# A fused attention and ELU kernel: relu from PSUM on VectorE, batch 2's exp tiles summed ahead of the row sums, and another order of the steps

## The chip, the cores and the metric

One NeuronCore of a Trainium2 chip runs the kernel. The metric is the device time of one execution in microseconds (us), smaller is better. The kernel before was run three times: 334.13, 334.70 and 338.02 us, median 334.7 us.

The core has these engines: TensorE (PE in the profile; its weight loads are PEld), VectorE (DVE), ScalarE (ACT), GpSimd (POOL) and SyncE (SP). PE multiplies from SBUF into PSUM. The others work on tiles of 128 partitions. POOL and SP issue the DMA transfers here. Each engine takes its instructions in the order in which they were issued to it.

## What is computed

Attention with 16 extra key and value rows per batch (the beacon), then a two-layer network with ELU over the result. Cut to what matters:

```python
# B, H, S, Nb, D = 8, 8, 576, 16, 64
k_all = np.concatenate([beacon_k, k], axis=2)
v_all = np.concatenate([beacon_v, v], axis=2)
scores = scale * np.matmul(q, k_all.transpose(0, 1, 3, 2))      # causal mask on the last S columns
a = np.exp(scores - scores.max(-1, keepdims=True))
a /= a.sum(-1, keepdims=True) + 1e-09
x = np.matmul(a, v_all).transpose(0, 2, 1, 3).reshape(B * S, H * D)   # 4608 x 512
h = x @ w_in                                                          # 4608 x 2048
g = np.where(h > 0.0, h, np.exp(np.minimum(h, 0.0)) - 1.0)            # ELU
out = g @ w_out                                                       # 4608 x 512
```

## The kernel before, in words

The kernel is a set of small functions, the steps, each marked `@step`, and one long string of step names that `run` (line 784) goes through from left to right. `F.2.11` calls `F(2, 11)`. A step only issues instructions. No scheduler moves them afterwards: the string is the order of every engine's queue, DMA queues included. Waits between engines follow from the data, from buffers that are used again, and from PSUM banks that two engines read.

**Attention**, per batch b (0 to 7) and pair p of heads (0 to 3). `lq` (line 247) loads q and k of batches 0 to 2 with POOL DMAs into the staging tiles `qst` and `kst`, of which there are two of each, taken in turn by even and odd batches. `T` transposes them on PE; `cq` and `ck` copy the result to SBUF on VectorE or ScalarE; `cb` puts the beacon's keys in front. From batch 3 on, `lk` (line 758) writes q and k in bf16 to a DRAM scratch, `lt` (line 763) brings them back transposed with SP DMAs, and `lp` (line 773) lets POOL write the beacon's keys into the same staging tile; `lp` therefore waits for the last reader of the batch that was in the tile before, and the POOL DMAs queued behind it wait with it. `lv` loads v, `wi` and `wo` load the two weights, all through POOL.

`S` computes transposed scores into PSUM, 512 columns a group; `x` (line 330) takes their exponential on ScalarE into the fp16 tile `et`; `m` multiplies masked blocks on VectorE. `L` (line 402) forms the row sums by multiplying `et` with a tile of ones: 20 matmuls of up to 464 columns over the five key blocks for the queries from 112 on, and 12 small ones for the first 112 queries and for half of their output. For batches 3 to 7 the step `D` (line 387) first adds the five key blocks of a pair of heads on VectorE, with four additions that shrink from 928 to 160 columns, into the `qk` tiles that `T` used before, and then `L` needs 4 matmuls in place of the 20. `n` turns the row sums into reciprocals on ScalarE (Ln, then Exp with scale -1), `W` multiplies with v, and `M` scales on VectorE into `xT`.

**Network.** Tokens are cut into tiles t: two of 256 tokens and eight of 512. `F` (line 503) multiplies `xT` with w_in into one PSUM bank `hps`, of which there are two in turn. The ELU of such a bank is done in one of two ways:

- `e`, `u`, `k`: ScalarE takes Exp of the bank (line 522) and Relu of the bank (line 527); VectorE forms min(exp - 1, relu) (line 537). This is ELU, as exp(h) - 1 is at least h.
- `e`, `r`, `g`: ScalarE takes Exp alone; VectorE forms min(exp, 1) - 1 in SBUF (`r`: line 545 for tiles 0 to 5, with a broadcast tile of ones, line 549 for tiles 6 and 7) and then the maximum with the bank in PSUM (`g`, line 554). This spares ScalarE the Relu.

`G` (tiles 0 and 1) and `Q` (tiles 2 to 9) multiply with w_out; `Q` uses Strassen's scheme, whose sums of weights and activations are `wt`, `H`, `Z` and, for the first product of tiles 8 and 9, `X`, `P`, `K`, `E`, `U` and `V`. `J` drains the sums from PSUM on either engine and writes the output through SP. `warm` and `wm` are matmuls on zeros, placed where PE has nothing to do yet.

Of the kernel before, what the change touches and what calls it, by code (L numbers as in the profile page):

```python
# [17 lines left out]
def kernel(  # L18
# [383 lines left out]
    def L(b, g):  # L402
# [12 lines left out]
        else:  # L415
            t = hd[b, g] = psum.tile([P, 1024], FP32, tag="S", name="lt")
            r_ = lt[b, g] = t[:, 512 - QA:512 - QA + S]
            if b >= BD:
                for i in range(4):
                    nc.tensor.matmul(  # L420
                        out=r_[32 * i:32 * (i + 1), QA:S], lhsT=ones,
                        rhs=presum[b, 2 * g + i // 2][:, i % 2, QA:S], start=True, stop=True, skip_group_check=True)
# [101 lines left out]
    @step  # L524
    def u(t, i):
        rb[t, i] = melt.tile([P, 512], FP16, tag="r", name="r")
        nc.scalar.activation(out=rb[t, i], in_=flat(hp[t, i]), func=AFT.Relu, bias=0.0, scale=1.0)  # L527
# [13 lines left out]
    @step  # L541
    def r(t, i):
        rb[t, i] = melt.tile([P, 512], FP16, tag="r", name="r")
        if t < 6:
            nc.vector.scalar_tensor_tensor(
                out=rb[t, i], in0=eb[t, i], scalar=1.0, in1=one32.to_broadcast([P, 512]),
                op0=ALU.min, op1=ALU.subtract)
# [393 lines left out]
```

## Time and profile before

| | us |
|---|---|
| median of three runs | 334.7 |
| profiled execution | 336.74 |
| its span, first to last instruction | 335.0 |
| DVE busy in it | 284.7 |
| ACT busy in it | 278.1 |
| POOL busy in it | 90.9 |

The profile is of one execution. Busy time is the time in which an engine worked on instructions; the end of a matmul in it is modelled. The page cuts the span in 40 slices of 8.4 us and shows the busy share in tenths. The chain of waits starts from the last instruction and follows back, at each step, to what released it. Groups collect instructions of one line with their mean duration; consecutive instructions of an engine overlap a little, so that a group's mean is slightly more than the step from one to the next. Of ELU steps, the kernel before has 120 `e`, of which 100 go on with `u` and `k` and 20 with `r` and `g`.

### The profile page before, as it was taken

The page shows a single profiled execution, that of the slowest core. Times are in us where ns is not written, and L with a number is a line of the kernel's source. Part 1 is how long each engine was busy: PE and PEld are TensorE (multiplying, and loading weights), DVE is VectorE, ACT ScalarE, POOL GpSimd, SP SyncE. Part 2 cuts the span into 40 slices and gives each one's busy share as a digit, 9 for nine tenths or more (in the row PEclk, how much of TensorE's full clock was granted, in tenths as well). Part 3 has the DMA queues.
Part 4 walks back from the last instruction along what each step waited for, and adds up shares of the span by engine and source line. Part 5 has one row for each costly group of instructions (what it writes and reads, how often), then busy time and mean ns, then how long its engine had stood idle before and what let it go on. Part 6 is the DMA issues. An engine that isn't in the chain of part 4 may idle for free.

```text
span 335.0 us, 8848 instructions
## 1 busy us (share of the span) xinstructions
PE 325.6 (97%) x3616; PEld 210.7 (63%) x3616; DVE 284.7 (85%) x601; ACT 278.1 (83%) x452; POOL 90.9 (27%) x117
## 2 busy tenths in 40 slices
...
GB/s 115 157 179 175 205 189 163 158 154 162 163 3 102 172 140 173 166 178 118 53 136 151 5 68 102 71 35 31 38 61 31 45 54 31 48 47 33 64 65 95
DMA packets 129113, 34.66 MB, mean 103 GB/s; under 512 B 112944, under 2 KB 127536, under 8 KB 129072
## 3 DMA queue, kind: packets, MB, share of 16 engines
...
## 4 chain that ended last, share of the span: by engine, by line
PE 87%; DVE 3%; ACT 3%; POOL 2%; DMA 2%; issue 1%; ACTq 0%; DVEq 0%; POOLq 0%
PE hps L512 30%; PE ops L627 29%; PE sc L321 8%; PE ut L378 6%; PE hps L697 5%; PE ops L563 4%; PE lt L378 2%; DMA kst<-in_k_dram 2%; ACT et L336 2%; POOL qst L136 1%; PE lt L420 1%; PE w L214 1%; PE tp L267 1%; PE ub L378 1%; DVE gt L554 1%
## 5 line engine op out<-in xcount | busy, mean ns | idle before, releaser
L512 PE MATMUL hps<-xT,w_in 128*128 128x512 f16 (+1 forms) x544 | 118.5, 354 | 0.3
L336 ACT ACTIVATE et<-sc 128x1024 f16<-128x1024 f32 (+2 forms) x114 | 105.7, 978 | 10.1 <-PE sc L321 9.5
L627 PEld LDWEIGHTS <-gt 128*128 128x128 f16 x768 | 73.3, 98 | 20.2 <-issue 3.7
L522 ACT ACTIVATE e<-hps 128x512 f32<-128x512 f32 x120 | 73.5, 620 | 13.8 <-PE hps L512 11.2
L512 PEld LDWEIGHTS <-w_in 128*128 128x128 f16 x544 | 50.6, 98 | 41.4 <-issue 4.4
L537 DVE SCALAR_TENSOR_TENSOR gt<-e,r 128x512 f16<-128x512 f32 x100 | 67.0, 684 | 8.0 <-ACT r L527 7.9
L527 ACT ACTIVATE r<-hps 128x512 f16<-128x512 f32 x100 | 61.9, 626 | 0.0
L627 PE MATMUL ops<-w_out,gt 128*128 128x256 f16 x384 | 50.7, 273 | 0.4 <-DVE gt L537 0.4
L627 PE MATMUL ops<-wt,gt 128*128 128x256 f16 x384 | 50.7, 273 | 0.0
L149 POOL DMA_DIRECT2D v<-in_v_dram x40 | 34.7, 919 | 5.0 <-DMA w_out<-in_moe_w_out_dram 2.7
L341 DVE TENSOR_TENSOR et<-et,triu 128x512 f16<-128x512 f16 (+4 forms) x108 | 31.2, 332 | 2.6 <-ACT et L336 2.4
L584 DVE TENSOR_TENSOR gt<-gt 128x1024 f16<-128x1024 f16 x48 | 32.4, 685 | 0.5
L378 PEld LDWEIGHTS <-v 128*32 128x32 f16 (+1 forms) x800 | 17.1, 96 | 10.6 <-issue 3.1
L394 DVE TENSOR_TENSOR qk<-qk,et 128x672 f16<-128x672 f16 (+2 forms) x60 | 21.2, 368 | 0.4
L378 PE MATMUL ut<-et,v 128*32 128x464 f16 (+3 forms) x560 | 20.9, 296 | 0.0
L472 DVE TENSOR_TENSOR xT<-ut,rl 128x672 f16<-128x672 f32 (+12 forms) x26 | 16.4, 670 | 3.1 <-PE ut L378 2.1
L643 DVE TENSOR_TENSOR osb<-ops,sm 128x512 f32<-128x512 f32 x24 | 16.4, 683 | 2.0 <-PE ops L627 1.9
L627 PE MATMUL ops<-w_out,s 128*128 128x256 f16 x128 | 17.1, 273 | 0.0
L563 PE MATMUL ops<-w_out,gt 128*128 128x512 f16 x64 | 16.0, 380 | 0.0
L736 DVE SCALAR_TENSOR_TENSOR gt<-e,r 128x512 f16<-128x512 f32 x24 | 15.9, 684 | 0.1
L627 PEld LDWEIGHTS <-s 128*128 128x128 f16 x128 | 12.3, 98 | 3.1 <-issue 0.3
L554 DVE TENSOR_TENSOR gt<-hps,r 128x512 f16<-128x512 f32 x20 | 13.7, 687 | 0.7
...
## 6 DMA issues: line engine op xcount, KB each, us to landing
...
```

The source lines that it names most:

```text
L149: nc.gpsimd.dma_start(out=vt[b][r0:r0 + n, j, :, :], in_=v[b, :, ilo[j]:ilo[j] + n, :].rearrange("h s d -> s h d"),)
L321: nc.tensor.matmul(out=s[:, h, a - c0:e - c0], lhsT=t[D * h:D * (h + 1), 1, P * j:P * (j + 1)], rhs=t[D * h:D * (h + 1), 0, NB + qa + a - ...
L336: nc.scalar.activation(out=ets[b, d][:, :, a - EC2 * d:e - EC2 * d], in_=sc[b, g][:, :, a - c0:e - c0], func=AFT.Exp, bias=0.0, scale=SCALE)
L341: nc.vector.tensor_tensor(out=o, in0=o, in1=i, op=ALU.mult)
L378: nc.tensor.matmul(out=t[32 * i:32 * (i + 1), a - qa:e - qa], lhsT=ones[0:kc[j], :] if half is None else v16[0:kc[j], j, h, 32 * half:32 * ...
L512: nc.tensor.matmul(out=h[:, n_, :], lhsT=w_in16[:, cc, P * fc:P * (fc + 1)], rhs=xt[k][:, cc, a - TT * k:e - TT * k], start=(cc == 0), sto ...
L522: nc.scalar.activation(out=eb[t, i], in_=flat(hp[t, i]), func=AFT.Exp, bias=0.0, scale=1.0)
L527: nc.scalar.activation(out=rb[t, i], in_=flat(hp[t, i]), func=AFT.Relu, bias=0.0, scale=1.0)
L537: nc.vector.scalar_tensor_tensor(out=half(t, i), in0=eb[t, i], scalar=1.0, in1=rb[t, i], op0=ALU.subtract, op1=ALU.min)
L563: nc.tensor.matmul(out=ob[t, tb_], lhsT=gt[:, fc, P * tb_:P * (tb_ + 1)], rhs=w_out16[:, fc, :], start=(fc == 0), stop=(fc == NFC - 1))
L584: (nc.vector if eng == "v" else nc.gpsimd).tensor_tensor(out=o_, in0=a_, in1=b_, op=op_)
L627: nc.tensor.matmul(out=xy[t, n_][:, qd, :], lhsT=lw[:, P * qd:P * (qd + 1)], rhs=wt_[:, c, :], start=(first and qd == 0 and c == 0), stop= ...
```

## The change

**The second way of ELU.** `u` gets an argument for its engine. With `.v`, VectorE takes the relu of the bank in PSUM, and `k` goes on as before. In the new order 31 of the 118 `u` carry `.v`; two `r` and `g` are left, on tile 6, where there were 20. The special form of `r` for tiles 0 to 5 goes, and its tile of ones with it.

**Batch 2's sums.** `L` takes the short form wherever `D` has been called for the pair. The order calls `D` for pairs 0 and 1 of batch 2, so that one of batch 2's two `L` has the short form.

**The order** is another one throughout. What the prediction speaks of: at the start POOL issues `ident` and all four `lq.0` before `lv.0.2`, where `lv.0.2` and `ident` stood between the first two and the last two; there are 14 `wm.4` in place of 18; `lq.2` stands behind `lv.1.2.3.4` and `lp.3.0`, where it stood right behind `wo.0`; of the `J` that copy or drain for Strassen's sums 6 are on VectorE in place of 11; one of batch 2's copies after the transposes moves from VectorE to ScalarE.

```diff
-    one32 = konst.tile([P, 1], FP32)
-    nc.vector.memset(one32, 1.0)
...
-            if b >= BD:
+            if (b, 2 * g) in presum:
...
     @step
-    def u(t, i):
+    def u(t, i, eng="s"):
         rb[t, i] = melt.tile([P, 512], FP16, tag="r", name="r")
-        nc.scalar.activation(out=rb[t, i], in_=flat(hp[t, i]), func=AFT.Relu, bias=0.0, scale=1.0)
+        if eng == "s":
+            nc.scalar.activation(out=rb[t, i], in_=flat(hp[t, i]), func=AFT.Relu, bias=0.0, scale=1.0)
+        else:
+            nc.vector.tensor_scalar(out=rb[t, i], in0=flat(hp[t, i]), scalar1=0.0, scalar2=None, op0=ALU.max)
...
     def r(t, i):
         rb[t, i] = melt.tile([P, 512], FP16, tag="r", name="r")
-        if t < 6:
-            nc.vector.scalar_tensor_tensor(
-                out=rb[t, i], in0=eb[t, i], scalar=1.0, in1=one32.to_broadcast([P, 512]),
-                op0=ALU.min, op1=ALU.subtract)
-        else:
-            nc.vector.tensor_scalar(
-                out=rb[t, i], in0=eb[t, i], scalar1=1.0, scalar2=1.0, op0=ALU.min, op1=ALU.subtract)
+        nc.vector.tensor_scalar(
+            out=rb[t, i], in0=eb[t, i], scalar1=1.0, scalar2=1.0, op0=ALU.min, op1=ALU.subtract)
...
     run("""
-    warm.4 warm.4 lq.0.0.0.4 lq.0.1.0.4 lv.0.2 warm.4 wm.4 ident T.0.0.0 bt ck.0.0.0 wm.4
-    T.0.1.0 bk cb.0.2 cb.0.0 wm.4 lq.0.0.4.8 S.0.0.0 x.0.0.0 lq.0.1.4.8 T.0.0.1 lq.1.0.0.4 tri
...
-    wm.4 x.0.1.1 T.0.2.1 S.0.3.0 wm.4 wm.4 x.0.3.0 T.0.3.1 cq.0.2.1 cq.0.3.1 S.0.2.0 wi.0
-    S.0.2.3 x.0.2.0 wm.4 wm.4 x.0.2.3 wm.4 wm.4 m.0.0.0 m.0.2.0 m.0.1.0 S.0.3.1 x.0.3.1 wm.4
...
-    x.0.2.2 M.0.A.0 M.0.A.1 F.0.2 e.0.2 u.0.2 k.0.2 lv.0.3.4 S.1.5 x.1.5 m.0.2.2 S.1.0 F.0.1
...
-    S.1.8 F.1.5 k.0.4 H.1.0 e.0.6 r.0.6 x.1.8 wo.0 lq.2.0.4.8 g.0.6 G.0.1.0 e.1.5 r.1.5 g.1.5
-    S.1.12 x.1.12 lq.2.0.0.4 wo.1 S.1.9 x.1.9 F.1.2 lv.1.0.1 S.1.10 x.1.10 F.1.3 m.1.2.1 cb.2.1
-    wo.2 e.1.3 T.2.2.0 u.1.3 cq.2.2.0 T.2.1.0 ck.2.1.0 G.0.0.0 e.1.2 u.1.2 T.2.0.0 lv.1.2.3.4
...
+    warm.4 lq.0.0.0.4 lq.0.1.0.4 warm.4 ident warm.4 wm.4 lq.0.0.4.8 wm.4 wm.4 bt bk lq.0.1.4.8
+    T.0.0.0 T.0.1.0 ck.0.1.0 cb.0.2 lv.0.2 lq.1.0.0.4 wm.4 cb.0.0 cb.0.1 lv.0.0.1 cb.0.3
...
+    tri cq.0.2.0 T.0.2.1 cq.0.2.1 S.0.3.0 x.0.3.0 T.0.3.1 cq.0.3.1 S.0.2.0 x.0.2.0 wm.4 S.0.2.3
+    wm.4 wm.4 m.0.0.0 m.0.2.0 x.0.2.3 S.0.2.1 x.0.2.1 S.0.3.1 x.0.3.1 m.0.1.0 wm.4 S.0.3.2
...
+    M.0.A.0 S.0.2.2 wi.0 M.0.A.1 F.0.2 m.0.0.2 u.0.2.v x.0.3.3 x.0.2.2 e.0.2 m.0.2.3 S.1.0 x.1.0
...
+    lv.1.2.3.4 u.1.5.v S.1.9 x.1.9 k.1.5 lp.3.0 cb.2.1 lq.2.0.0.4 F.1.2 S.1.10 x.1.10 u.1.2.v
+    cb.2.3 e.1.2 F.1.3 lq.2.0.4.8 T.2.2.0 m.1.2.0 T.2.1.0 G.0.0.0 e.1.3 ck.2.1.0 cq.2.2.0 H.1.2
...
+    e.2.14 S.2.8 F.2.0 wt.4.0 D.2.0.0 x.2.8 F.2.9 u.2.0 e.2.0 k.2.0 u.2.9 e.2.9 G.0.0.3 lp.3.1
...
     """)
```

More of the change, by code (lines that the diff above doesn't have):

```diff
@@ new lines @@
+    T.2.0.0 T.2.3.0 wo.1 u.1.3 F.0.7 m.1.2.1 ck.2.0.0 k.1.3 ck.2.3.0 u.0.7.v G.0.0.1 S.2.0 S.2.1
+    m.1.3.0 x.2.0 x.2.1 m.1.0.1 k.1.2 m.1.1.0 m.1.3.1 G.0.1.1 m.1.0.0 F.1.0 wo.3 u.1.0.v S.2.3
+    e.0.7 lv.1.0.1 L.1.0 e.1.0 x.2.3 F.1.6 k.0.7 H.1.0 L.1.1 n.1.0 M.1.0.0 e.1.6 m.2.0.0 n.1.1
+    k.1.0 M.1.1.0 wo.2 G.0.1.2 cb.2.2 u.1.6 W.1.1 M.1.1.1 W.1.0 S.2.2 x.2.2 G.0.0.2 M.1.0.1
+    F.2.11 e.2.11 H.2.2 u.2.11.v k.1.6 F.2.6 e.2.6 lv.2.0.1 S.2.4 x.2.4 u.2.6.v S.2.5 k.2.11
+    x.2.5 F.2.8 e.2.8 lk.3.0 u.2.8.v wt.1.0 lk.3.1 k.2.6 F.2.14 u.2.14 wt.2.0 k.2.8 G.0.1.3
@@ new lines @@
+    G.1.0.1 F.2.3 S.3.1 e.2.3 W.2.0 x.3.1 S.3.4 wt.2.1 m.2.3.1 k.2.4 u.2.3 x.3.4 M.2.0.1 k.2.3
+    F.2.10 F.2.12 e.2.10 e.2.12 L.2.1 lv.3.0.1 u.2.10.v u.2.12 o.0.1 k.2.10 S.3.8 n.2.1 x.3.8
+    F.2.7 k.2.12 F.2.5 M.2.1.0 W.2.1 u.2.7.v S.3.2 u.2.5 e.2.5 Z.2.3.0 M.2.1.1 e.2.7 Q.2.0.7
+    x.3.2 F.3.5 lk.4.0 k.2.7 e.3.5 s.0.1 k.2.5 m.3.1.0 u.3.5.v Z.2.1.0 k.3.5 S.3.6 S.3.9 F.3.2
+    lk.4.1 F.3.8 x.3.6 e.3.2 m.3.0.1 x.3.9 u.3.2.v G.1.0.2 lp.4.0 S.3.5 x.3.5 Z.2.3.1 lt.4.0
+    lt.4.1 e.3.8 S.3.10 x.3.10 k.3.2 Q.2.7.14 Z.2.1.1 lv.3.2.3.4 G.1.0.3 u.3.8 S.3.0 F.3.1 o.1.0
@@ new lines @@
+    lk.5.0 x.3.0 e.3.1 F.3.0 D.3.1.0 S.3.12 x.3.12 S.3.11 u.3.1 x.3.11 s.0.0 m.3.0.0 Q.2.14.21
+    Q.2.21.28 J.2.0 lk.6.1 wt.3.1 u.3.0 k.3.8 F.3.14 Z.2.2.0 S.4.1 u.3.14 Z.2.2.1 Z.2.4.0 e.3.0
+    S.4.0 D.3.0.0 e.3.14 D.3.0.1 H.1.1 Q.2.28.35 Q.2.35.42 J.2.1 k.3.0 Z.2.4.1 Q.2.42.49 k.3.1
+    D.3.0.2 F.3.6 D.3.0.3 x.4.1 x.4.0 u.3.6 m.3.1.1 D.3.1.1 e.3.6 F.3.4 k.3.6 J.2.2.v Q.2.49.56
+    S.3.7 lp.4.1 e.3.4 D.3.1.2 u.3.4 k.3.4 m.3.3.0 x.3.7 m.3.3.1 m.3.2.0 S.4.3 F.3.9 e.3.9
+    k.3.14 u.3.9 wt.4.1 D.3.1.3 wt.3.0 x.4.3 Q.2.56.63 F.3.15 e.3.15 u.3.15 k.3.15 F.3.3 S.4.4
@@ new lines @@
+    x.4.4 e.3.3 W.3.0 L.3.0 u.3.3 n.3.0 D.3.3.0 D.3.3.1 Q.2.63.70 J.2.3 m.3.2.1 F.3.7 e.3.7
+    k.3.3 u.3.7 Q.2.70.77 Q.2.77.84 D.3.3.2 F.3.11 e.3.11 F.3.12 M.3.0.1 D.3.3.3 Q.2.84.91 k.3.9
+    J.2.4 u.3.11 S.4.12 u.3.12 M.3.0.0 e.3.12 x.4.12 D.3.2.0 Z.3.3.0 D.3.2.1 k.3.12 D.3.2.2
+    D.3.2.3 S.4.11 x.4.11 F.3.13 e.3.13 k.3.7 Q.2.91.98 F.3.10 L.3.1 J.2.5 u.3.13 k.3.13 n.3.1
+    k.3.11 M.3.1.0 W.3.1 M.3.1.1 m.4.3.1 Q.2.98.105 lk.5.1 F.4.3 e.3.10 m.4.1.0 S.4.2 lt.5.0
+    u.3.10 e.4.3 k.3.10 u.4.3.v Z.3.3.1 S.4.10 Q.2.105.112 J.2.6.v F.4.8 x.4.10 Z.3.1.1 x.4.2
@@ new lines @@
+    e.4.8 u.4.8.v F.4.6 e.4.6 k.4.3 S.4.6 Z.3.1.0 x.4.6 k.4.8 S.4.5 x.4.5 Q.3.0.7 u.4.6 lp.5.0
+    Q.3.7.14 Q.3.14.21 S.4.7 S.5.4 Z.3.2.1 Z.3.2.0 x.5.4 m.4.0.0 x.4.7 F.4.7 F.4.9 k.4.6 J.3.0
+    Q.3.21.28 u.4.9.v e.4.7 u.4.7.v m.4.0.1 e.4.9 k.4.7 Q.3.28.35 S.5.2 m.4.1.1 J.3.1 H.2.1
+    S.4.9 x.5.2 F.4.1 D.4.0.0 Z.3.4.0 x.4.9 F.4.2 u.4.1 e.4.1 u.4.2 e.4.2 D.4.0.1 Q.3.35.42
+    k.4.9 S.5.0 lk.6.0 S.5.3 m.4.3.0 Q.3.42.49 x.5.0 lt.6.0 F.4.4 x.5.3 Q.3.49.56 e.4.4 lt.5.1
+    k.4.1 F.4.5 k.4.2 J.3.2 S.4.8 lv.4 u.4.4.v S.5.1 lp.7.0 e.4.5 k.4.4 x.4.8 D.4.1.0 D.4.1.1
@@ new lines @@
+    D.4.0.2 D.4.1.2 Z.3.4.1 D.4.0.3 m.4.2.1 D.4.1.3 lp.5.1 u.4.5 k.4.5 x.5.1 m.5.0.0 F.4.10
+    m.4.2.0 u.4.10 Q.3.56.63 Q.3.63.70 F.4.12 u.4.12 L.4.0 S.5.5 D.4.3.0 Q.3.70.77 e.4.12 x.5.5
+    n.4.0 F.4.14 D.4.2.0 e.4.14 m.5.0.1 J.3.3 D.4.2.1 M.4.0.0 u.4.14 D.4.2.2 W.4.0 M.4.0.1 S.5.6
+    x.5.6 Q.3.77.84 F.4.15 e.4.10 S.5.10 k.4.12 x.5.10 D.4.3.1 u.4.15 D.4.2.3 W.4.1 D.4.3.2
+    m.5.1.1 D.4.3.3 k.4.10 e.4.15 L.4.1 n.4.1 D.5.0.0 J.3.4 D.5.0.1 m.5.1.0 F.4.0 e.4.0 M.4.1.1
+    M.4.1.0 Q.3.84.91 Q.3.91.98 D.5.0.2 D.5.1.0 J.3.5 F.4.13 u.4.0 S.5.12 x.5.12 k.4.0 S.5.7
@@ new lines @@
+    lp.6.0 x.5.7 e.4.13 Q.3.98.105 F.5.6 S.6.1 D.5.1.1 S.6.4 u.5.6 Q.3.105.112 k.4.14 k.4.15
+    lp.6.1 D.5.1.2 x.6.1 Q.4.0.7 lt.6.1 H.4.1 u.4.13.v J.3.6.v k.4.13 S.5.9 Q.4.7.14 D.5.0.3
+    F.4.11 m.5.2.0 e.5.6 Z.4.3.0 x.5.9 x.6.4 e.4.11 u.4.11.v F.5.11 k.4.11 D.5.1.3 S.5.8 Z.4.3.1
+    S.5.11 Q.4.14.21 x.5.8 Z.4.1.0 J.4.0 F.5.7 Z.4.1.1 lv.5 W.5.0 e.5.11 x.5.11 u.5.11 k.5.6
+    Z.4.2.1 lk.7.1 u.5.7 k.5.11 e.5.7 Z.4.2.0 m.5.3.0 H.2.0 k.5.7 lv.6 L.5.0 n.5.0 M.5.0.1 F.5.1
+    u.5.1 e.5.1 F.5.14 Q.4.21.28 k.5.1 e.5.14 Q.4.28.35 M.5.0.0 J.4.1 u.5.14 F.5.15 e.5.15
@@ new lines @@
+    S.6.0 Z.5.3.1 e.5.3 x.6.0 S.6.10 F.5.9 u.5.9.v x.6.10 D.6.1.0 Q.4.98.105 e.5.9 m.6.0.0
+    D.6.0.0 F.5.0 S.6.8 u.5.0 e.5.0 x.6.8 S.6.6 m.6.0.1 D.6.0.1 k.5.0 k.5.3 k.5.9 Q.4.105.112
+    x.6.6 m.6.1.1 F.6.6 F.6.11 e.6.11 u.6.11 e.6.6 u.6.6 Z.5.1.1 J.4.6 Q.5.0.7 Q.5.7.14 S.6.11
+    x.6.11 F.6.4 Z.5.3.0 k.6.11 D.6.1.1 k.6.6 e.6.4 u.6.4 Q.5.14.21 S.7.2 Z.5.1.0 k.6.4 x.7.2
+    S.6.12 F.6.5 e.6.5 u.6.5 D.6.1.2 x.6.12 m.6.3.0 F.6.15 e.6.15 J.5.0.v Q.5.21.28 Z.5.2.0
+    u.6.15 Q.5.28.35 S.7.4 x.7.4 S.6.7 x.6.7 F.6.7 J.5.1 e.6.7 u.6.7 m.6.3.1 F.6.14 k.6.15
@@ new lines @@
+    m.6.2.1 D.6.0.2 D.6.0.3 W.6.0 D.6.1.3 L.6.0 H.4.0 e.6.14 u.6.14 Z.5.2.1 Q.5.35.42 m.6.2.0
+    Z.5.4.0 k.6.14 k.6.5 n.6.0 M.6.0.0 M.6.0.1 k.6.7 F.6.9 e.6.9 u.6.9 F.6.10 e.6.10 Q.5.42.49
+    k.6.9 J.5.2.v Q.5.49.56 S.7.1 u.6.10 x.7.1 D.6.3.0 S.7.3 x.7.3 Z.5.4.1 F.6.3 e.6.3 F.6.0
+    e.6.0 u.6.0 Q.5.56.63 r.6.3 g.6.3 m.7.1.0 m.7.0.1 S.7.6 x.7.6 S.7.5 Q.5.63.70 F.6.8 D.6.2.0
+    x.7.5 k.6.0 e.6.8 u.6.8 F.6.1 e.6.1 u.6.1 k.6.8 J.5.3 S.7.0 x.7.0 k.6.1 S.7.9 D.6.2.1
+    D.6.3.1 D.6.3.2 D.6.2.2 F.6.13 e.6.13 u.6.13 Q.5.70.77 F.6.12 k.6.13 D.6.2.3 Q.5.77.84 F.6.2
@@ new lines @@
+    e.6.12 D.6.3.3 r.6.12 J.5.4 L.6.1 x.7.9 k.6.10 n.6.1 e.6.2 M.6.1.0 u.6.2 W.6.1 Q.5.84.91
+    Q.5.91.98 Q.5.98.105 g.6.12 Z.6.3.1 M.6.1.1 F.7.15 F.7.0 Q.5.105.112 e.7.15 J.5.5 m.7.0.0
+    lv.7 u.7.15 S.7.7 D.7.1.0 e.7.0 S.7.12 F.7.3 m.7.1.1 k.6.2 x.7.7 Q.6.0.7 D.7.0.0 u.7.0
+    Z.6.3.0 J.5.6 D.7.1.1 Z.6.1.0 x.7.12 Q.6.7.14 D.7.0.1 F.7.12 k.7.0 Q.6.14.21 e.7.3 u.7.3
+    D.7.1.2 J.6.0 e.7.12 S.7.11 u.7.12 S.7.10 x.7.10 k.7.3 F.7.10 F.7.2 Z.6.1.1 k.7.12 Q.6.21.28
+    e.7.10 u.7.10 k.7.15 Z.6.2.0 D.7.0.2 D.7.0.3 e.7.2 u.7.2 Z.6.2.1 s.1.0 k.7.2 Q.6.28.35
@@ new lines @@
+    D.7.1.3 x.7.11 F.7.7 Z.6.4.1 F.7.13 e.7.7 u.7.7 m.7.3.0 L.7.0 k.7.7 e.7.13 u.7.13 k.7.13
+    S.7.8 F.7.8 F.7.1 x.7.8 e.7.1 m.7.3.1 D.7.3.0 Q.6.35.42 J.6.1 Q.6.42.49 m.7.2.0 D.7.2.0
+    u.7.1 k.7.1 m.7.2.1 Q.6.49.56 Q.6.56.63 e.7.8 F.7.6 u.7.8 k.7.8 n.7.0 J.6.2 e.7.6 Q.6.63.70
+    Z.6.4.0 F.7.4 k.7.10 u.7.6 D.7.3.1 D.7.3.2 k.7.6 M.7.0.0 e.7.4 F.7.14 u.7.4 D.7.3.3
+    Q.6.70.77 F.7.5 J.6.3.v Q.6.77.84 k.7.4 e.7.14 D.7.2.1 u.7.14 e.7.5 u.7.5 Z.7.3.0 F.7.9
+    D.7.2.2 e.7.9 D.7.2.3 k.7.14 F.7.11 L.7.1 u.7.9 n.7.1 e.7.11 J.6.4 Z.7.3.1 u.7.11 W.7.0
@@ new lines @@
+    H.3.1 P.8.0.0 K.8.0.0 H.3.0 Q.6.84.91 Q.6.91.98 k.7.9 X.8.1 Q.6.98.105 k.7.5 P.8.0.1 M.7.1.0
+    X.8.2 k.7.11 X.8.4 P.8.0.2 Q.6.105.112 K.8.0.2 J.6.6 K.8.0.1 P.8.0.3 X.8.3 P.8.0.4 M.7.0.1
+    Q.7.0.7 K.8.0.3 K.8.0.4 J.6.5 U.8.0.1 E.8.0.1 U.8.0.4 P.8.0.5 P.8.0.6 E.8.0.6 Z.7.1.0
+    K.8.0.5 Q.7.7.14 E.8.0.4 U.8.0.6 Z.7.2.0 Q.7.14.21 J.7.0 P.8.1.0 K.8.1.0 V.8.0.6 P.8.1.1
+    Q.7.21.28 P.8.1.2 E.8.0.5 K.8.1.2 V.8.0.1 K.8.1.1 V.8.0.4 E.8.1.1 Z.7.1.1 Q.7.28.35 P.8.1.3
+    U.8.0.5 Z.7.2.1 P.8.1.4 Z.7.4.0 K.8.1.3 K.8.1.4 W.7.1 P.8.1.5 U.8.1.1 P.8.1.6 V.8.1.1 J.7.1
@@ new lines @@
+    U.8.1.6.v K.8.1.5 V.8.0.5 E.8.1.6 V.8.1.6 H.3.2 Q.7.35.42 Q.7.42.49 U.8.1.4 E.8.1.4 P.8.2.0
+    P.8.2.1 Q.7.49.56 K.8.2.0 K.8.2.1 P.8.2.2 Q.7.56.63 J.7.2 K.8.2.2 P.8.2.3 P.8.2.4 U.8.1.5.v
+    Q.7.63.70 E.8.2.1 U.8.2.1.v Z.7.4.1 E.8.1.5 V.8.2.1 K.8.2.3 P.8.2.5 K.8.2.4 Q.7.70.77
+    K.8.2.5 J.7.3 U.8.2.4 P.8.2.6 E.8.2.6 V.8.1.5 U.8.2.6 V.8.1.4 M.7.1.1 F.8.13 e.8.13 u.8.13
+    V.8.2.6 E.8.2.4 X.9.1 X.9.3 k.8.13 X.9.2 Q.7.77.84 F.8.15 e.8.15 u.8.15 k.8.15 F.8.12 e.8.12
+    u.8.12 J.7.4 k.8.12 Q.7.84.91 Z.8.3.0 V.8.2.4 F.8.14 e.8.14 P.9.0.0 K.9.0.0 Q.7.91.98
@@ new lines @@
+    Q.7.98.105 u.8.14 E.8.2.5 k.8.14 P.9.0.1 K.9.0.1 P.9.0.2 U.8.2.5 Q.7.105.112 K.9.0.2 U.9.0.1
+    J.7.5 V.8.2.5 P.9.0.3 Z.8.1.0 Q.8.0.7 X.9.4 P.9.0.4 K.9.0.3 P.9.0.5 J.7.6 K.9.0.4 E.9.0.1
+    U.9.0.4 K.9.0.5 Q.8.7.14 P.9.0.6 E.9.0.6 U.9.0.6 Z.8.3.1 P.9.1.0 K.9.1.0 Q.8.14.21 Q.8.21.28
+    E.9.0.4 Z.8.1.1 P.9.1.1 V.9.0.1 Z.8.2.0 Z.8.2.1 P.9.1.2 J.8.0 U.9.0.5 K.9.1.1 Q.8.28.35
+    V.9.0.4 J.8.1 V.9.0.6 Q.8.35.42 E.9.0.5 P.9.1.3 K.9.1.2 U.9.1.1 K.9.1.3 P.9.1.4 K.9.1.4
+    E.9.1.1 V.9.0.5 Q.8.42.49 Q.8.49.56 E.9.1.4 U.9.1.4 P.9.1.5 J.8.2 V.9.1.1 P.9.1.6 K.9.1.5
@@ new lines @@
+    V.9.1.4 Z.8.4.1 U.9.1.5.v Q.8.56.63 E.9.1.6 U.9.1.6 F.9.12 Z.8.4.0 E.9.1.5 e.9.12 V.9.1.5
+    P.9.2.0 V.9.1.6 u.9.12 Q.8.63.70 Q.8.70.77 P.9.2.1 K.9.2.0 k.9.12 P.9.2.2 J.8.3 Q.8.77.84
+    K.9.2.2 K.9.2.1 E.9.2.1 P.9.2.3 P.9.2.4 Z.9.3.0 K.9.2.3 U.9.2.1 Q.8.84.91 J.8.4 Q.8.91.98
+    P.9.2.5 K.9.2.4 U.9.2.4 V.9.2.1 J.8.5 E.9.2.4 P.9.2.6 U.9.2.6 K.9.2.5 Q.9.0.7 E.9.2.6
+    E.9.2.5 Z.9.1.0 V.9.2.4 F.9.13 U.9.2.5.v e.9.13 V.9.2.6 u.9.13 V.9.2.5 k.9.13 F.9.14 e.9.14
+    Q.8.98.105 u.9.14 F.9.15 Q.8.105.112 e.9.15 u.9.15 k.9.14 Q.9.7.14 Z.9.3.1 J.8.6 Q.9.14.21
```

137 lines of the change are left out of this document (24 added, 113 removed).

## The prediction

> **What bounds the kernel now.** I read the busy line and the slices first, then the engines stretch by stretch, then the chain of waits at its start, and last the groups that the change touches.
>
> ```profile
> PE 325.6 (97%) x3616; PEld 210.7 (63%) x3616; DVE 284.7 (85%) x601; ACT 278.1 (83%) x452; POOL 90.9 (27%) x117
> ```
> ```profile
> 0.00:20.00 20.00, 16.96 (x220) 10.38 (x220) 9.95 (x35) 9.62 (x12) 16.09 (x31) 0.91 1.26 145
> 20.00:40.00 20.00, 18.90 (x408) 13.89 (x406) 10.30 (x26) 19.93 (x31) 13.77 (x22) 1.00 1.23 184
> ...
> 60.00:80.00 20.00, 19.96 (x224) 9.22 (x212) 15.44 (x34) 17.20 (x28) 7.17 (x5) 1.00 2.09 164
> 80.00:100.00 20.00, 20.00 (x252) 9.93 (x249) 15.15 (x33) 19.20 (x31) 0.85 (x2) 1.00 0.86 94
> 100.00:120.00 20.00, 20.00 (x185) 11.20 (x186) 19.77 (x44) 19.77 (x32) 11.78 (x15) 1.00 1.39 131
> ```
>
> The columns are PE, PEld, DVE, ACT and POOL busy, then granted clock, DMA share and GB/s. From 60 to 300 us PE works all the time. There a lighter ScalarE or an earlier relu buys nothing by itself: only fewer or cheaper matmuls do, and PE can only lose. What can be won otherwise lies before 60 us. There ScalarE is full from 20 to 40 us, and before that it waits. The chain of waits (start, length, what) says for what:
>
> ```profile
> 8.59 6.19 DMA kst<-in_k_dram
> ...
> 17.23 1.82 PE w L214 x16
> ...
> 19.55 3.89 ACT et L336 x5
> ...
> 27.95 0.98 PE hps L512 x8
> ...
> 57.84 0.92 PE lt L378 x32
> ...
> 119.96 0.20 PE lt L420 x4
> 120.16 0.15 PE lt L378 x12
> ```
>
> The set-up hangs on the landing of k's last part at 14.8 us, then on 16 warming matmuls, then on the exponentials. The last three lines are a row sum with and without `D`. The groups of the ELU steps, by form:
>
> ```profile
> L537 DVE SCALAR_TENSOR_TENSOR gt<-e,r 128x512 f16<-128x512 f32 x100 | 67.0, 684 | 8.0 <-ACT r L527 7.9
> L554 DVE TENSOR_TENSOR gt<-hps,r 128x512 f16<-128x512 f32 x20 | 13.7, 687 | 0.7
> L545 DVE SCALAR_TENSOR_TENSOR r<-e,one 128x512 f16<-128x512 f32 x14 | 9.6, 688 | 2.6 <-ACT e L522 2.4
> L728 DVE TENSOR_SCALAR r<-hps 128x512 f16<-128x512 f32 x1 | 0.7, 692 | 0.5 <-ACT e L719 0.5
> ```
>
> The last one is a relu from PSUM on VectorE, the operation that the change adds 31 times; it began when ScalarE's Exp of the same bank had ended.
>
> **The start.** In the chain k's last DMA is issued at 8.59 us, behind `lv.0.2` (0.57 us for the beacon rows, 0.90 us for the other). These go behind it: it is issued 1.47 us earlier. The transfers themselves are full from 5 us on (nine tenths or more of every slice), so the gain may be only the 144 KB that no longer stand ahead, at 150 GB/s 0.95 us. So 1.0 to 1.5 us. ScalarE's idle times between its first exponential and its first Ln are 1.84 us (this landing), 0.55 us and 1.02 us (both behind warming matmuls: 8 and 16 of them stood between the groups of scores, now none and 8). Against this stands that the first group waits for a copy that moved to VectorE behind four small ones of 0.08 us each, 0.3 us. Of 3.41 us I take 2.4 as gained, bounds 1.5 and 3.1. From there ScalarE is busy without a gap up to 46 us in the trace, and carries the gain to the first `F` (27.9 us, now 25.5). The weights allow that: the last of the eight DMAs of `wi.0`, issued at 19.81 us, landed 4.9 us later, at 24.7. PE could follow: 16 warming matmuls at 0.08 us (8 took 0.62) are 1.3 us less work, at the half clock of that moment (16 in 1.82) up to 1.8.
>
> **POOL's queue after it.** `lq.2` now stands behind `lp.3.0`, which may write only when PE has transposed batch 1's last pair (39.8 us, ended 40.3; shifted by 2.4, 37.9). `lp` took 0.35 to 1.25 us in the trace, four `lq` DMAs 0.67 us each. The last is issued at about 40.5 us. A 288 KB part of k landed 7.4 us after its issue at 28 us and 12.7 us after one at 32.1 us, where others were queued ahead. With the lighter queue (`wo.0` landed at 39.0, then 352 KB of v, then four parts that landed 1.45 us apart before) it comes at 46.6 to 48.4 us. Batch 2's first transposes, 49.9 us before, ask for it at 47.5. So the stall is 0 to 0.9 us, 6 with the longest landing; I take 0.5. Behind it `wo.1`, `wo.3`, `lv.1.0.1` and `wo.2` shift alike: at the 2.6 us that a w_out part took to land after the one before, `L.1.0` and `G.0.1.2` get theirs about 1.5 us before they ask. No charge, bound 1 us.
>
> **PE's work from the first `F` on.** `L.2.0` falls from the 0.92 us of 32 matmuls to 0.20 + 0.15: 0.57 us. Groups of scores stand in 67 runs in place of 69; PE lost some 0.1 us at each change between scores and other work (7 matmuls of `Q` took 0.87 us behind scores, 0.77 behind `F`): 0.2 us. F, Q, G, W and P are the same in number. Sum 0.8 us less.
>
> **The ELU steps.** `r` and `g` cost VectorE 0.688 + 0.687 us, relu and `k` cost 0.692 + 0.684: the same to a hundredth. The bank is free after the first of the two and not after both, 0.69 us earlier; PE did not wait for banks after 60 us, so this is worth nothing there. What costs is that the sparing way is used more often. VectorE: 31 relus (21.5 us) and 18 more `k` (12.3), less 18 `g` (12.4), 14 `r` at 0.688 and 4 at 0.420 (11.3), plus `D` for two pairs (2 x (0.634 + 0.500 + 0.369 + 0.234) = 3.5), less five `J` (3.4), one copy (1.35) and 0.8 of `U`: 8.0 us more. ScalarE: 13 relus less (8.1), five `J`, two `U` and one copy more (5.4): 2.8 us less. By tiles, 7.7 us of VectorE's come with tiles 0 to 2, before 105 us, where it idles 9.4 us from 60 to 100 alone; 1.7 come with tiles 3 to 7, where the stretches from 100 to 300 sum to 190.5 of 200. That a VectorE 99% busy need not hold PE, the stretch from 100 to 120 us shows: 19.77 of 20, and PE 20.00. So between 0 and 3 us; I take 1.0, near the lower end, because that row is the nearest to what tile 2 becomes (30.6 + 5.6 of 40 us).
>
> **The end.** The last 105 matmuls (11.8 us) follow VectorE's `k` of tile 9's last banks, and this chain keeps its steps; one block of seven matmuls fewer lies behind the last `F`. 0, bounds -0.3 and +0.8.
>
> **Sum:** -2.4 + 0.5 - 0.8 + 1.0 = -1.7 us. The profiled execution took 336.74 us (span 335.0) and becomes 335.0; it was 2.0 us above the median of the runs, so the median goes from 334.7 to 333.0 us.
>
> **The rivals.**
>
> *POOL's wait (slower).* The price of `lq.2` behind `lp.3.0` is what I set at 0.5 us. If its last part lands more than 2.2 us after 47.5 us, the gain is gone and the kernel is slower; with the 12.7 us row it lands at 53.2, a stall of 5.7 us: 334.7 - 2.2 + 5.7 = 338.2. For it speaks that the transfers are the fullest resource up to 60 us; against it, that the 12.7 us row had 0.5 MB of w_out more ahead of it.
>
> *ScalarE held by VectorE.* Exp and relu of a bank go one after the other in the program, and in 10 of the 31 tiles the relu is first. Then ScalarE waits for VectorE, with all exponentials queued behind. Five of these lie before 60 us, where ScalarE has nothing to give: at 0.69 us each, 3.5 us: 334.7 - 1.7 + 3.5 = 336.5. Against it: VectorE has 9.7 us idle from 20 to 40 us, so that it may be done before ScalarE comes. The Trainium skill, PSUM — Partial Sum Buffer, section "PSUM bank collisions raise a hardware error", says that two engines may not read one bank at once and that software must put a wait between them; by that rule none of the 31 pairs overlaps, and the relu at 314.09 us, 0.50 us of idle behind Exp, agrees.
>
> *VectorE becomes the bound* from 57 to 90 us: `D`, the seven relus and the moved weight sums fall together, and its waits for ScalarE (7.9 us before `k`) don't shrink. If 3 us more of idle stay than I assume: 336.
>
> *More comes of the start:* all 3.4 us of ScalarE's gaps and no stall: 334.7 - 3.4 - 0.8 = 330.5.
>
> *It doesn't do what it says:* ScalarE is spared 2.8 us where nobody waits for it, and k lands no earlier since the transfers were full: 334.5.
>
> **How the numbers follow.** Forecast 0.40, POOL 0.15, ScalarE held 0.13, VectorE 0.12, more from the start 0.10, nothing 0.10. The likeliest case alone is 332 to 334.2. The range takes in the rivals up to POOL's, and their runs' spread: 330.5 to 338.0. 2% (6.7 us, about what a measurement of this kernel can tell from no change) is more than any case gives on the fast side, as PE's work sets the floor; on the slow side it needs two rivals at once, or a wait later in the order. Faster 0.04, within 0.86, slower 0.10.
>
> **What would show it.** In the profile after: first `F` at 25.5 us; no idle time of 1.84 us in ScalarE's first exponentials; batch 2's first transposes near 47.5 us with under 1 us of waiting for `qst` or `kst`; the relus at 0.69 us; VectorE at 36 of 40 us from 60 to 100; PE 20.00 in each stretch from 100 to 300. PE waits for VectorE or SP's transposes after 100 us, or a first `F` at 27 us, would make the prediction wrong.

## The result and the profile after

The changed kernel takes 338.44 us (median of 20 runs, 336.57 to 339.79), the kernel before 334.95 (20 runs on the same chips). The ratio is 1.0081, 95% interval 1.0057 to 1.0104: slower by 0.8%, where 0.5% faster was forecast, and 0.4 us above the upper end of the range. The profiled execution took 337.08 us, its span 335.4.

The busy line of the changed kernel and its stretches (columns PE, PEld, DVE, ACT, POOL busy, then granted clock, DMA share, GB/s):

```profile
PE 323.0 (96%) x3584; PEld 209.3 (62%) x3584; DVE 290.8 (87%) x613; ACT 276.6 (82%) x447; POOL 89.2 (27%) x117
```
```profile
20.00:40.00 20.00, 19.27 (x391) 14.02 (x391) 14.33 (x34) 18.49 (x28) 12.95 (x23) 1.00 1.27 160
40.00:60.00 20.00, 17.08 (x249) 11.33 (x251) 15.83 (x35) 16.48 (x23) 15.49 (x16) 1.00 1.56 180
60.00:80.00 20.00, 19.80 (x213) 9.36 (x206) 16.27 (x33) 16.80 (x28) 9.45 (x10) 1.00 2.09 154
80.00:100.00 20.00, 20.00 (x239) 9.61 (x238) 18.83 (x42) 17.64 (x28) 7.04 (x5) 1.00 2.25 172
100.00:120.00 20.00, 20.00 (x174) 11.19 (x176) 19.07 (x42) 19.21 (x31) 7.11 (x8) 1.00 1.52 146
```

PE is busy 2.6 us less than in the profile before (323.0 against 325.6 us), and part of that is the granted clock of 0.91 that the profile before shows in its first 20 us. PE stands 2.9 us from 40 to 60 us. VectorE and ScalarE are idle there too: nobody is the bound in that stretch, somebody waits. The timeline of the changed kernel around it (start, length, engine, line, operation; in brackets the idle time just before and what ended it):

```profile
41.47 0.63 ACT L520 ACTIVATE e<-hps 128x512 f32<-128x512 f32 x1
42.13 0.69 DVE L528 TENSOR_SCALAR r<-hps 128x512 f16<-128x512 f32 x1 [0.37 <-ACT e L520]
42.86 0.69 DVE L538 SCALAR_TENSOR_TENSOR gt<-e,r 128x512 f16<-128x512 f32 x1
43.47 0.56 DVE L339 TENSOR_TENSOR et<-et,triu 128x512 f16<-128x512 f16 x2
43.95 0.68 DVE L528 TENSOR_SCALAR r<-hps 128x512 f16<-128x512 f32 x1
44.66 0.60 ACT L520 ACTIVATE e<-hps 128x512 f32<-128x512 f32 x1 [2.56 <-DVE r L528]
45.16 1.94 ACT L334 ACTIVATE et<-sc 128x1024 f16<-128x1024 f32 x2
46.23 0.40 PE L319 MATMUL sc<-hi 64*128 64x224 bf16 x6 [2.22 <-ACT et L334]
47.14 0.40 PE L319 MATMUL sc<-hi 64*128 64x96 bf16 x8 [0.52 <-ACT et L334]
```

Read it from the bottom. PE's scores `S.1.12` wait 2.22 us for a bank that ScalarE empties with the exponentials `x.1.11` and `x.1.8` (45.16). These are queued behind `e.1.4` (44.66), which stood 2.56 us behind VectorE's relu of the same bank, `u.1.4.v` (43.95). In the order the relu is named first. VectorE came to it late, since ahead of it stood `u.0.6.v` (42.13, itself waiting for the exponential that began at 41.47), `k.0.6` (42.86) and two masks (43.47). The bank itself had been full since 41.6 us, where the profile ends the matmuls of `F.1.4`.

This is not all of the loss. Of the 20 runs four had a mean granted clock of 1.000 (336.57 to 337.08, the profiled one among them), and 16 had 0.988 to 0.995, at 337.85 to 339.79, 1.9 us later by the medians. The experiments show what that is.

### The profile page after: what moved, and what is told of

Same layout as the page of the kernel before. It is cut to its first block, busy times and chain, and to the rows that moved or that the text cites. A ratio compares the mean times of both kernels' runs of the same rounds, so it can differ in the third digit from the quotient of the medians.

```text
span 335.4 us, 8767 instructions
## 1 busy us (share of the span) xinstructions
PE 323.0 (96%) x3584; PEld 209.3 (62%) x3584; DVE 290.8 (87%) x613; ACT 276.6 (82%) x447; POOL 89.2 (27%) x117
## 4 chain that ended last, share of the span: by engine, by line
PE 85%; DVE 4%; POOL 4%; DMA 3%; ACT 2%; issue 1%; ACTq 0%; POOLq 0%
PE ops L623 30%; PE hps L510 29%; PE sc L319 7%; PE ut L376 6%; PE hps L693 6%; PE ops L559 4%; DMA v<-in_v_dram 2%; PE lt L376 2%; DVE r L528 1%; ACT et L334 1%; DMA w_in<-in_moe_w_in_dram 1%; POOL qst L136 1%; PE lt L418 1%; DVE gt L538 1%; POOL kst L136 1%
## 5 line engine op out<-in xcount | busy, mean ns | idle before, releaser
L538 DVE SCALAR_TENSOR_TENSOR gt<-e,r 128x512 f16<-128x512 f32 x118 | 79.6, 684 | 3.3 <-ACT r L526 2.1
L526 ACT ACTIVATE r<-hps 128x512 f16<-128x512 f32 x87 | 53.8, 624 | 2.5 <-PE hps L510 2.3
L623 PE MATMUL ops<-w_out,gt 128*128 128x256 f16 x384 | 49.1, 273 | 0.0
L149 POOL DMA_DIRECT2D v<-in_v_dram x40 | 37.2, 1130 | 1.8 <-DMA qst<-in_q_dram 1.1
L528 DVE TENSOR_SCALAR r<-hps 128x512 f16<-128x512 f32 x31 | 21.3, 688 | 9.7 <-ACT e L520 7.4
L392 DVE TENSOR_TENSOR qk<-qk,et 128x672 f16<-128x672 f16 (+2 forms) x66 | 23.5, 367 | 0.4
L773 POOL COPY qst<-bkT 128x32 bf16<-128x32 bf16 x5 | 2.5, 508 | 51.7 <-PE sc L319 51.5
L732 DVE SCALAR_TENSOR_TENSOR gt<-e,r 128x512 f16<-128x512 f32 x24 | 15.9, 685 | 0.0
```

What stands on the lines that cost most here:

```text
L149: nc.gpsimd.dma_start(out=vt[b][r0:r0 + n, j, :, :], in_=v[b, :, ilo[j]:ilo[j] + n, :].rearrange("h s d -> s h d"),)
L528: nc.vector.tensor_scalar(out=rb[t, i], in0=flat(hp[t, i]), scalar1=0.0, scalar2=None, op0=ALU.max)
L538: nc.vector.scalar_tensor_tensor(out=half(t, i), in0=eb[t, i], scalar=1.0, in1=rb[t, i], op0=ALU.subtract, op1=ALU.min)
L623: nc.tensor.matmul(out=xy[t, n_][:, qd, :], lhsT=lw[:, P * qd:P * (qd + 1)], rhs=wt_[:, c, :], start=(first and qd == 0 and c == 0), stop= ...
```

## The experiments

Times are medians; every run goes against the kernel before on the same chip (334.8 to 335.0 us in each case).

| kernel | us | ratio to before, 95% interval |
|---|---|---|
| changed kernel | 338.44 | 1.0081 (1.0057 to 1.0104) |
| `e.1.4` ahead of its relu | 334.67 | 0.9984 (0.9959 to 1.0008) |
| `x.1.11` ahead of `e.1.4` | 337.35 | 1.0047 (1.0019 to 1.0074) |
| `lq.2` ahead of `lp.3.0` | 338.00 | 1.0081 (1.0051 to 1.0111) |
| before, relu in place of r and g | 334.51 | 0.9988 (0.9953 to 1.0023) |
| changed, `F.1.5` three times | 337.08 | 1.0042 (1.0012 to 1.0071) |
| `e.1.4` first, no D of batch 2 | 335.06 | 0.9991 (0.9966 to 1.0016) |
| before, with D of batch 2 | 336.00 | 1.0023 (0.9993 to 1.0053) |
| all ten exponentials moved ahead | 339.70 | 1.0136 (1.0090 to 1.0181) |
| `e.1.4` first, nine relus moved back | 336.43 | 1.0026 (0.9998 to 1.0054) |
| `u.1.4` on ScalarE | 334.73 | 0.9981 (0.9956 to 1.0005) |
| the same, `F.1.2` earlier | 335.34 | 1.0001 (0.9981 to 1.0021) |

**One exponential, one place earlier.**

```diff
-    m.1.1.1 u.1.4.v e.1.4 x.1.11
+    m.1.1.1 e.1.4 u.1.4.v x.1.11
```

> The changed kernel with e.1.4 one place earlier, ahead of VectorE's relu of the same bank. Theory (ScalarE held by a relu that stands first): e.1.4 follows e.0.6 at about 42.1 us instead of 44.66, the exponentials behind it start 2.5 us earlier, PE's waits of 2.2 + 0.5 us for ScalarE's score tiles at 46 to 47 us fall below 0.5 us in sum, and the median falls from 338.4 to about 336 us. Rival (VectorE has too much to do before 60 us, and the order of the two does not matter): VectorE's queue behind u.1.4 gets 0.6 us later and PE stands as long; 338 to 339 us. Rival (half-clock stretch at the start): 338.4, no change.

334.67 us: 3.8 us less than the changed kernel, where some 2.4 were expected. The exchange of two words takes back the whole loss. Its timeline:

```profile
41.83 1.12 ACT L520 ACTIVATE e<-hps 128x512 f32<-128x512 f32 x2
42.79 2.00 ACT L334 ACTIVATE et<-sc 128x1024 f16<-128x1024 f32 x2
44.31 0.93 PE L319 MATMUL sc<-hi 64*128 64x224 bf16 x14
44.32 0.68 DVE L528 TENSOR_SCALAR r<-hps 128x512 f16<-128x512 f32 x1
```

The two ELU exponentials run back to back, the score exponentials follow at 42.79 instead of 45.16, and PE's scores have no wait in brackets. VectorE's relu runs where it ran before (44.32, in a run whose first `F` came 0.4 us later): VectorE is as late as it was, and nothing that PE needs waits for it.

**Only ScalarE's order changed.**

```diff
-    u.1.4.v e.1.4 x.1.11 wo.0
+    u.1.4.v x.1.11 e.1.4 wo.0
```

> The changed kernel with ScalarE's x.1.11 ahead of e.1.4; VectorE's order is untouched. Theory (ScalarE held): x.1.11 runs at about 42.1 us while VectorE makes its relu, ScalarE's idle time of 2.56 us shrinks to about 1.5 us, PE's wait of 2.2 us at 46 us is gone or below 0.7 us, and the median falls by 1.5 to 2.7 us, to 336 to 337. Rival (VectorE overloaded): 338.4 as before. Rival (half-clock stretch at the start): 338.4.

337.35 us, 1.1 less and just outside the 336 to 337 expected. PE no longer waits at `S.1.12`, but now 1.90 us at `S.1.9`, whose bank `x.1.8` empties, and that still stands behind `e.1.4`; ScalarE idles 1.65 us:

```profile
44.49 0.60 ACT L520 ACTIVATE e<-hps 128x512 f32<-128x512 f32 x1 [1.65 <-DVE r L528]
46.05 0.40 PE L319 MATMUL sc<-hi 64*128 64x96 bf16 x8 [1.90 <-ACT et L334]
```

7 of the 12 runs had a clock of 0.991 to 0.995, the others (335.5 to 336.5) 0.997 to 1.000. The wait went with the place of `e.1.4`, as the theory has it, but less of it than expected.

**POOL's queue.**

```diff
-    lp.3.0 cb.2.1 lq.2.0.0.4 F.1.2 S.1.10 x.1.10 u.1.2.v
-    cb.2.3 e.1.2 F.1.3 lq.2.0.4.8
+    lq.2.0.0.4 lq.2.0.4.8 lp.3.0 cb.2.1 F.1.2 S.1.10 x.1.10 u.1.2.v
+    cb.2.3 e.1.2 F.1.3
```

> The changed kernel with all four lq.2 DMAs ahead of lp.3.0 on POOL's queue. Theory (ScalarE held): batch 2's transposes did not wait for their loads, so 338.4 within 0.7 us. Rival (POOL's queue): their q and k parts come up to 0.9 us earlier, and the time falls by 0.9 us or more.

338.0: 0.4 us less, within the 0.7 us expected; the rival is out. Its profile caught what most runs have and the changed kernel's own did not. PE by the microsecond (PE busy, granted clock, DMA share, GB/s):

```profile
43.00:44.00 1.00, 0.84 (x8) 1.00 1.34 212
44.00:45.00 1.00, 0.00 (x0) 1.00 1.26 201
45.00:46.00 1.00, 0.00 (x0) 1.00 1.24 205
46.00:47.00 1.00, 0.42 (x8) 0.81 1.27 210
47.00:48.00 1.00, 1.00 (x11) 0.50 1.20 200
48.00:49.00 1.00, 1.00 (x7) 0.50 1.26 215
49.00:50.00 1.00, 1.00 (x7) 0.50 1.66 179
50.00:51.00 1.00, 1.00 (x12) 0.98 2.30 163
```

PE stands from 43.8 to 46.1 us, works for 0.4 us and stands for 0.5 us more; from 46.6 us on it is granted half its clock for 3.4 us. At half clock that costs up to 1.7 us once more: half of 3.4 us is 0.5% of the span, which fits the 0.995 of 14 of the sixteen runs.

**Does the clock follow the wait?** PE computes `F.1.5` three times, with the same result: 16 matmuls more, in the hole.

> The changed kernel in which PE computes F.1.5 three times over (16 matmuls, 2.1 us more work, the same result), just ahead of the scores for which it waits 2.2 us; ScalarE keeps its wait. Theory (ScalarE's wait makes PE stand idle, and the idle PE then gets half the clock for 3.4 us in most runs, as in the profiles of the two runs with x.1.11 moved and lq.2 moved): the filler fits into the wait, no half-clock stretch follows, and the median falls by about 1.6 us, from 338.4 to about 336.8. Rival (the clock has nothing to do with the wait): 338.4, or up to 340.5 if the filler does not fit.

337.08 us: with 1.7 us more work for PE (24 matmuls in 2.78 us, where 8 take 1.04) the kernel is 1.4 us faster, and none of the 12 runs has a clock under 0.997. The wait of ScalarE is as before; PE's row is full up to 46 us and keeps its clock behind it:

```profile
44.00:45.00 1.00, 1.00 (x11) 1.00 1.22 177
45.00:46.00 1.00, 1.00 (x12) 1.00 1.30 194
46.00:47.00 1.00, 0.52 (x8) 1.00 1.31 186
47.00:48.00 1.00, 0.48 (x14) 1.00 1.05 150
```
```profile
45.29 0.60 ACT L520 ACTIVATE e<-hps 128x512 f32<-128x512 f32 x1 [2.57 <-DVE r L528]
```

So 3.8 us of loss are about 2.1 us of standing (336.77, the median of the changed kernel's four runs at a clock of 1.000, less 334.67) and 1.7 us of half clock.

**The queue or the work?** The relu of that bank goes to ScalarE (`u.1.4.v` becomes `u.1.4`).

> The changed kernel with the relu of tile 1's bank 4 on ScalarE, still ahead of e.1.4; VectorE loses one relu. Theory (it was the wait for VectorE's queue, where the relu stood behind e.0.6's relu, its k and two masks, not the relu's work): the relu runs at about 42.1 us, e.1.4 at 42.8 in place of 44.66, PE's wait of 2.2 us is gone to below 0.7 us, no half-clock stretch; 334.7 to 335.5 us. Rival (ScalarE itself is the bound there): its 0.6 us more cost as much as the wait, 337 us or more.

334.73 us: 0.65 us more work for ScalarE costs nothing against 2.56 us of waiting. `e.1.4` runs at 42.16, and 0.52 us are left of PE's wait:

```profile
42.16 0.66 ACT L520 ACTIVATE e<-hps 128x512 f32<-128x512 f32 x1
44.70 0.40 PE L319 MATMUL sc<-hi 64*128 64x96 bf16 x8 [0.52 <-ACT et L334]
```

**The operation alone.** In the kernel before, the 14 pairs of `r` and `g` in tiles 1 to 5 become `u.v` and `k` in place.

> The kernel before, with only the operation changed: its 14 r and g pairs of tiles 1 to 5 become relu and k in the same places, the exponential ahead of the relu everywhere, the order otherwise untouched. Theory (it is the place of the relu, not the relu): the same to 0.5 us as the kernel before, 334.5 to 335.5 us; the relus from PSUM take 0.69 us. Rival (the relu from PSUM costs by itself, by a wait for the bank or a dearer instruction): 0.3 us and more above it, and the dearer groups show in the profile. Rival (the bank is free 0.69 us earlier, and that is worth something): faster by over 0.3 us.

334.51 us, the same. The relu group of this kernel (mean 688 ns) is as dear as the min that it replaces (688 ns in the kernel before):

```profile
L530 DVE TENSOR_SCALAR r<-hps 128x512 f16<-128x512 f32 x14 | 9.6, 688 | 2.8 <-ACT e L522 2.5
```

That the bank comes free 0.69 us earlier shows no gain here. This run also shows what the start of the kernel before looks like when no half-clock stretch falls into it (its chain of waits):

```profile
7.06 4.76 DMA kst<-in_k_dram
...
15.52 5.40 ACT et L336 x7
...
25.04 0.04 issue
25.08 0.35 PE sc L321 x4
25.43 0.98 PE hps L512 x8
```

Its first `F` starts at 25.4 us, and at 25.6 in the profile of the kernel before with D, which has the same start. The changed kernel's starts at 25.2, in the profiles of the other kernels with its start at 24.8 to 25.8. In the profiled execution of the kernel before it was 27.9. PE from 16 to 20 us (PE busy, granted clock, DMA share, GB/s), first in that execution, then in this run:

```profile
16.00:18.00 2.00, 2.00 (x37) 0.57 2.06 173
18.00:20.00 2.00, 2.00 (x22) 0.58 1.20 203
```
```profile
16.00:18.00 2.00, 2.00 (x49) 1.00 1.79 184
18.00:20.00 2.00, 1.51 (x26) 1.00 1.12 206
```

**D of batch 2 taken out, and put in alone.**

> The kernel with e.1.4 ahead of its relu (334.67 us), and batch 2's exp tiles not summed: L.2.0 computes its row sums from all key chunks again. Theory (D of batch 2 pays on PE and is hidden on VectorE): PE has 0.57 us more, the median rises to about 335.2. Rival (VectorE is the bound from 60 to 90 us, so that the 3.5 us of D cost more than they bring): it falls by 0.3 us or more.

> The kernel before with batch 2's exp tiles of pairs 0 and 1 summed on VectorE, between m.2.1.0 and L.2.0, and nothing else changed. Theory (PE's work is the bound there): 0.57 us less, about 334.2 us. Rival (VectorE's 3.5 us more delay banks and masks there): no change or slower, up to 336.5.

The first experiment takes `D` out of the changed order (with `e.1.4` first), the second puts it into the kernel before. Taking it out costs 0.4 us by the medians, near the 0.57 expected; but the runs of the two kernels overlap (334.1 to 335.5 and 334.7 to 335.5 us), so that a gain from `D` is likely and not shown. Put into the kernel before, ahead of `L.2.0`, it makes that 1.1 us slower. PE's row sum then waits for the last sum on VectorE:

```profile
82.44 0.37 PE L420 MATMUL lt<-qk,ones 128*32 128x464 f16 x2 [1.58 <-DVE qk L394]
```

My placing of it, close ahead of `L.2.0`, is part of that price; a better one was not tried. The profile of the changed order has no such wait.

**All ten relus that stand first.** First the exponentials were moved to where the relus stood:

> The changed kernel with the exponential ahead of VectorE's relu in all ten tiles where the relu was first. Theory (only e.1.4 held PE up; the others cost ScalarE 1.3 us before 60 us, of which PE sees 0.2 to 0.5): 334.2 to 334.8 us, no more than 0.5 us below the kernel with e.1.4 alone. Rival (every relu that is first costs its 0.69 us): 2 us and more below it, 332.5 us.

Both missed: 339.7 us, 5 us slower than with `e.1.4` alone. `e.0.2` had been moved ahead of two score exponentials, but now waits for PE's first `F`, and they with it; then PE waits for them:

```profile
25.86 0.60 ACT L520 ACTIVATE e<-hps 128x512 f32<-128x512 f32 x1 [1.42 <-PE hps L510]
27.26 0.39 PE L319 MATMUL sc<-qk 64*128 64x512 bf16 x2 [1.44 <-ACT et L334]
```

PE's listed waits from 20 to 300 us sum to 5.1 us, against 1.4 with `e.1.4` alone. In the profiled execution half clock follows (0.50 from 28 to 30 us), but three of the five runs had a clock of 0.999 or more and took 339.3 to 339.7 us, so the median is not made by it:

```profile
26.00:28.00 2.00, 0.39 (x2) 0.95 1.06 174
28.00:30.00 2.00, 1.99 (x13) 0.50 1.07 187
```

So the edit tested ScalarE's order as well. Cleaner: ScalarE's order stays, and the nine relus go behind their exponentials (`u.0.2.v x.0.3.3 x.0.2.2 e.0.2` becomes `x.0.3.3 x.0.2.2 e.0.2 u.0.2.v`, and so on).

> The kernel with e.1.4 ahead of its relu (334.67 us), and the nine other relus that stood first put right behind their exponentials; ScalarE's order stays as it is, VectorE's relus come later. Theory (only where ScalarE came to the bank before VectorE did could a relu that stands first hold it; there that was 1.3 us of ScalarE in all before 60 us, of which PE saw 0.2): 334.2 to 335.2, the same as with e.1.4 alone. Rival (every relu that is first costs): 1 us or more faster, 333.7 or less. Rival (a relu moved behind holds VectorE's queue, and PE through it): 335.5 or more.

336.43 us, 1.8 slower than with the nine relus first. The theory's number is missed and the last rival holds: a relu that comes later holds PE's next `F`. After 60 us PE waits for relus in four places, 1.1 us in sum, against 0.2 us in one place with the nine first. The longest is at 98 us, behind `u.2.7`:

```profile
98.09 1.02 PE L510 MATMUL hps<-xT,w_in 128*128 128x512 f16 x4 [0.56 <-DVE r L528]
```

The rest of the 1.8 us is in no single wait of the profile. So of the ten relus that stand first one is wrong; the other nine are better first as a group. None of the nine was moved alone.

**A try for more.** On top of `u.1.4` on ScalarE, `F.1.2` goes ahead of `S.1.9` (`u.1.5.v S.1.9` becomes `u.1.5.v F.1.2 S.1.9`), where PE still waited 0.52 us for ScalarE.

> The kernel with tile 1's relu of bank 4 on ScalarE (334.73 us), and PE's F.1.2 one group of scores earlier, between S.1.12 and S.1.9, where PE still waited 0.52 us for ScalarE's exponential of an earlier group. Theory (PE is the bound and its waits are what is left): the 0.52 us is filled, 334.2 to 334.4 us, under both kernels. Rival (S.1.9 and the exponentials behind it come 1 us later, and PE waits for S.1.10's buffers or for F.1.3's bank instead): 334.7 or more.

335.34 us: the rival holds. PE waits 0.62 us at `S.1.10` instead, and, in this profile, 0.90 us for a part of k (`kst`) at 48.75 us. No version beat the kernel before by more than the runs' uncertainty.

## Why the prediction was wrong

*What bounds the kernel.* Right: in the changed kernel PE is at 20.00 from 80 to 300 us, and what made it slow lies before.

*The start, -2.4 us: the first step that failed.* The signs that it named came: first `F` at 25.2 us (25.5 foretold), no gap of 1.84 us in ScalarE's first exponentials. But the kernel before has its first `F` at 25.4 and 25.6 us as well, in the two other profiled executions with its start. The landing of k at 14.8 us, the warming matmuls at half clock and the 27.9 belonged to the one profiled execution, which stood 2.0 us above the median; by these profiles that is the reason. The prediction notes the 2.0 us, and then takes a gain made of them off the median. What is left by the first `F` is some 0.3 us (25.5 on the mean of two profiles, 25.2 of ten) in place of 2.4. No run has the new start alone. What the new start may bring is the tail: 10 of the 35 runs of the kernel before beside the first experiments took over 336 us at a clock of 0.989 to 0.995, while none of the 72 runs with the changed start and without the long hole (`e.1.4` first, the filler, no D, nine relus back, `u.1.4` on ScalarE, and the same with `F.1.2` earlier) had a clock under 0.996.

*POOL's queue, +0.5 us.* 0 in the changed kernel: PE is late itself, and batch 2's first transposes come at 49.9 us. Without the standing, with `u.1.4` on ScalarE, they come at 47.4, where 47.5 was foretold, and wait for no load either. That the load lands close by is shown by the 0.90 us in the last experiment.

*PE's work, -0.8 us.* Nothing speaks against it: `D`'s part was 0.57, and taking `D` out cost 0.4, within the spread of the runs. The 0.2 us for the groups of scores was not tested.

*The ELU steps, +1.0 us: the second step that failed, and the one that turned the sign.* What it priced came near what was foretold: relu 0.688 us, VectorE busy 35.1 of 40 us from 60 to 100 (36 foretold), PE 20.00 from 80 us on. (In all VectorE is busy 6.1 us more and not 8.0, ScalarE 1.5 less and not 2.8; the sums were made of group means, which count the overlap of neighbours.) With `e.1.4` first PE idles 1.9 us from 20 to 80 us, in the kernel before with relus 0.75. Of these 1.2 us the profile puts 0.4 us, in two waits, down to relus; the rest it does not split. So the term itself is 0.4 to 1.2 us. What it put at nothing and left to a rival, ScalarE held by VectorE, came on top with 3.8 us. The rival named the mechanism and counted `u.1.4` among its five, at a chance of 0.13, and sized it wrongly. It charged each relu at its own length, 0.69 us. The length that counts is what VectorE has queued ahead of the relu when ScalarE arrives: 2.56 us in one place, and 1.1 us in two others together from 27 to 62 us. What was set against it, 9.7 us of idle VectorE from 20 to 40 us, was a sum over a stretch, not at the place, and the place lies after 40. And PE's wait was charged once, where the clock charges it again.

*Two readers of one bank, and the clock.* `e.1.4` begins 0.03 us after its relu ends: the two go one after the other. That agrees with the page of the Trainium skill that the prediction cites, PSUM — Partial Sum Buffer, section "PSUM bank collisions raise a hardware error". As for the clock, holes of 1.90 us (`x.1.11` moved) and 2.22 us (`lq.2` moved) stood ahead of 3.4 us at half clock in the profiles, and 16 of 20 runs of the changed kernel, whose profile has a hole of 2.22 us, had a clock of 0.995 or less. The Trainium skill, TensorE: Matmul & The Clock Gate, section "HAM oscillation — how this bites in real kernels", names gaps over some 3.4 us as those that bring the half clock; by its figure it would not have come here. The length of the half-clock stretch, 3.4 us, agrees with the page's window.

*The sum again.* With the start at -0.3, POOL at 0, PE at -0.8 and ELU at +0.4 to +1.2 it comes to -0.7 to +0.1 us; the kernel with `e.1.4` first stands 0.1 us under the kernel before (334.67 against 334.81), and its interval takes in both ends. To this the changed kernel adds the 3.8 us.
